# Ten of forty-eight input loads sent as two transfers over uneven parts of the partitions

## The chip, the cores and the metric

The kernel runs on one core of one Trainium2 chip. The metric is the time on the device in microseconds (us), the median over several runs. The core has a matrix engine (PE, with its weight loads, PEld), a vector engine (DVE), a scalar engine (ACT), GpSimd (POOL) and a sequencer, SyncE (SP), that here does nothing but issue transfers. Transfers between the chip's memory and the on-chip memory (128 partitions) are moved by 16 DMA engines.

## What is computed

Two layers in a row: a linear attention with a decaying state (RWKV-6), and a token mixer (HyperMixer) on its output. Batch 4, 8 heads, 768 steps, head size 48; the model width is 8 x 48 = 384.

```
for t in range(S):
    cur = einsum('bhd,bhe->bhde', u[None] * kt, vt)
    y[:, :, t] = einsum('bhd,bhde->bhe', rt, state + cur)
    state = wt[:, :, :, None] * state + einsum('bhd,bhe->bhde', kt, vt)
...
x = y.transpose(0, 2, 1, 3).reshape(B, S, H * D)
W_tok = einsum('bsd,btd->bst', x @ w_q, x @ w_k) / sqrt(d_hyper)
out = maximum(einsum('bst,btd->bsd', W_tok, x), 0.0) @ w_out
```

The four large inputs r, k, v and w (the decay) have the shape (4, 8, 768, 48) in float32, 4.7 MB each; the output is 4.7 MB too.

## The kernel before

The 768 steps of each batch are cut into three units of 256 steps, so there are twelve units, numbered n = 0 to 11; each unit is two chunks of 128. For a unit the kernel needs four inputs: w, k, r and v. Each is loaded by one transfer of 384 KB, so there are 4 x 12 = 48 input loads. A load puts two neighbouring steps on each of the 128 partitions: per partition it moves 8 heads x 2 steps x 48 values, in 8 runs of 384 bytes (two neighbouring steps of a head lie together in memory). The tiles `wg`, `kg`, `rg` and `vg` are rings of four buffers each, so a load may start when the unit four before it has been read from that buffer.

The readers of the loads are: ACT, which takes the logarithm of `wg` (`f_ln`, L378); GpSimd, at times ACT, which casts `kg` and `rg` to 16 bits (`cast16`, L384, recorded under L389); and GpSimd and ACT, which cast `vg` in four quarters into `VB` (`f_V`, L488, recorded under L493). Behind these casts PE transposes k and r, builds the products of each chunk (A), which DVE masks (`AM`, L535), updates the state (`SB`), and forms the unit's output; GpSimd multiplies the values for the present step (`Vd`, L515). After the third unit of a batch the token mixer runs on its rows, and the results are stored.

The order of work is written out by hand: `Plan.add` collects steps, the list `ORDER` says in which order they are issued, and each engine runs its own steps in that order. A step that waits holds all later steps of its engine. All input loads, the weights (`wts`, `wo`) and nearly all stores are issued by SyncE, in the order of `ORDER`. Of the input loads that is: w0 k0 r0 v0 w1 k1 r1 w2 v1 r2 k2 w3, then k4 k3 r3 v2 v3 w4 r4 w5 k5 v4, then, after the weights for q and k, r5 w6 k6 v5 and so on to v11. Each issue on SyncE takes the next of eight semaphores in turn, and waits until the transfer that used this semaphore before it has landed. The small input u is loaded by ACT in two transfers of 4 partitions each (L289).

The load itself is one statement of `load` (L223), called for each unit from the loop at L371. Its argument `e` is the way that the plan hands to a step; for loads it isn't used.

Of the kernel before, what the change touches and what calls it, by code (L numbers as in the profile page):

```python
# [17 lines left out]
def view(t, off, dims, p0=0, pn=128):  # L18

    base = t[ds(p0, pn), ds(off, 1)]  # L20
    return dataclasses.replace(base, ap=[list(base.ap[0])] + [list(d) for d in dims])
# [11 lines left out]
class Plan:  # L33
# [9 lines left out]
    def add(self, key, ways, fn, after=(), buf=None, reads=(), cols=0, mode=0, behind=None,  # L43
            half=-1, more=None):
        s = dict(key=key, ways=ways, way=ways[0], fn=fn, after=list(after), buf=buf,
                 reads=list(reads), cols=cols, mode=mode, behind=behind, half=half,
                 more=more or {}, i=len(self.steps), fills=False, out=False)
        if buf is not None:
            if buf.filler is None:
                buf.filler = s  # L50
                s["fills"] = True
                if buf.tile is None:
                    self.banks.append(buf)
                elif behind is None and buf.before is not None:
                    s["behind"] = buf.before.filler
            elif behind is None:
                s["behind"] = buf.filler
        self.steps.append(s)
        return s
# [77 lines left out]
WARM = 24  # L137
VSW = "PAD"
TURN = (9, 10)


@with_exitstack
def kernel(
# [12 lines left out]
    nc = tc.nc  # L156
    B, H, S, D = r.shape
    C = 128
    U = 2 * C
    NU = S // U  # L160
    NCH = S // C
    NP = H // 2
    D2 = 2 * D
# [56 lines left out]
    km = const([C, 1], F32, "km")  # L220

    def load(b, i, tl, ap, e):
        nc.sync.dma_start(  # L223
            out=view(tl, 0, [[D2, H], [1, D2]]),
            in_=ap[b, :, ds(i * U, U)].rearrange("h (p j) d -> p h (j d)", j=2))

    def pads(e, x):
        y = nc.vector if e == "D" else nc.gpsimd
# [7 lines left out]
    def ring(kind):  # L236
        x = Buf(kind, tiles[kind][used[kind] % RINGS[kind][0]])
        x.before = last.get(kind)
        last[kind] = x
        used[kind] += 1  # L240
        return x
# [7 lines left out]
    def either():  # L249
        return Buf("x")  # L250

    def at(b, dtype=F32):
        x = PS[:, ds(b.bank * 512, 1024 if b.kind == "w" else 512)]
        return x if dtype == F32 else x.bitcast(dtype)

    def copy(e, o, i, by=None):
        if e == "A":
            if by is None:
                nc.scalar.copy(o, i)  # L259
            else:  # L260
                nc.scalar.activation(o, i, ACT.Copy, bias=0.0, scale=by)
        else:
            x = nc.gpsimd if e == "P" else nc.vector
            if by is None:
                x.tensor_copy(o, i)  # L265
            else:
                x.tensor_scalar_mul(o, i, by)
# [56 lines left out]
    def dma(key, fn, after=(), buf=None, reads=()):  # L324
        return add(key, "S", fn, after, buf, reads)
# [35 lines left out]
    def unit(n, batch):  # L361
        b, i = divmod(n, NU)
# [7 lines left out]
        g = {}  # L370
        for name, ap in (("wg", w), ("kg", k), ("rg", r), ("vg", v)):  # L371
            g[name] = ring(name)
            g[name + "L"] = dma((name, n), lambda e, ap=ap, x=g[name].tile: load(b, i, x, ap, e),
                                buf=g[name])

        lw = ring("lw")
# [42 lines left out]
        for cs in fine:  # L419
# [7 lines left out]
            def f_en(e, cs=cs):  # L427
# [3 lines left out]
            x = add(("ep", n, cs[0]), "A", f_ep, [cws, su["kp"]], ep, [cw], cols=w_,  # L431
                    half=-1 if len(cs) > 1 else cs[0])
# [34 lines left out]
        for cs in fine:  # L467
# [7 lines left out]
            def f_KT(e, cs=cs):  # L475
# [3 lines left out]
            x = add(("RT", n, cs[0]), "D", f_RT, [rTs] + [eps[c] for c in cs] + new("ep"), RT, [rt, ep],  # L479
                    cols=512 * len(cs), half=half)  # L480
# [31 lines left out]
        for cs in fine:  # L512
# [5 lines left out]
            x = add(("Vd", n, cs[0]), "PD" if end else "P", f_vd, VBs + [dds], Vd, [VB, dd], cols=len(cs) * DM)  # L518
# [23 lines left out]
        for cs in ([(0,)] if final else fine):  # L542
            def f_kb(e, cs=cs):
                for c in cs:
# [10 lines left out]
            x = add(("kb", n, cs[0]), "eE" if kb.kind == "x" else "E", f_kb,  # L555
                    [KTs[c] for c in cs], kb, [KT], cols=len(cs), mode=dict(e=1, E=0))

            def f_kd(e, cs=cs):
# [3 lines left out]
                else:  # L562
                    x = view(at(kb, BF16), cs[0] * NP * D, [[D, n4], [1024, 2], [1, D]])
                copy(e, view(kd.tile, 64 + cs[0] * 1024, [[256, n4], [128, 2], [1, D]]), x, UNIT)
            x = add(("kd", n, cs[0]), "AD", f_kd, [x] + ([wts["pads"][n]] if n < 2 else []), kd,
                    [kb], cols=DM * len(cs))
# [81 lines left out]
        for p, cs in enumerate(each if end else both):  # L648
# [14 lines left out]
            def f_x(e, c0=c0, nc_=nc_, y=y):  # L663
# [5 lines left out]
                else:  # L669
# [4 lines left out]
                     more=dict(D=([Vds[c] for c in cs], [Vd]), A=([yv], [])))  # L674
            xt, XT = None if n in TURN else either(), ring("XT")

            def f_xt(e, c0=c0, nc_=nc_, xt=xt):
                for dt in range(NK):
                    for k_ in range(nc_):
# [5 lines left out]
                        for hf in range(2):  # L685
                            rows = ds(hf * 64, 64)
                            mm(at(xt, BF16)[:, ds(hf * 1024 + (k_ * NK + dt) * 64, 64)],
                               X.tile[rows, x], ID16[rows, rows], trans=True)
            if n not in TURN:
                xts = add(("xt", n, c0), "eE", f_xt, [xs], xt, [X], cols=nc_, mode=dict(e=1, E=0))  # L690

            def f_XT(e, nc_=nc_, xt=xt, XT=XT):
                if xt.kind == "s":
                    copy(e, XT.tile[:, ds(0, nc_ * DM)], at(xt, BF16)[:, ds(0, nc_ * DM)])
                else:
                    copy(e, view(XT.tile, 0, [[C, NK * nc_], [64, 2], [1, 64]]),
                         view(at(xt, BF16), 0, [[64, NK * nc_], [1024, 2], [1, 64]]))
            if n in TURN:
                XTs = dma(("XT", n, c0), lambda e, XT=XT: nc.sync.dma_start_transpose(
# [24 lines left out]
            if not end:  # L724
                def f_qk(e, f_wk=f_wk, f_wq=f_wq):
# [3 lines left out]
                x = add(("QK", n), "AD", lambda e, qk=qk: copy(  # L729
                    e, QK.tile[:, ds(i * QS, QS)], at(qk)[:, ds(0, QS)]), [qs], QK, [qk], cols=256)  # L730
# [86 lines left out]
    for n in range(N):  # L817
        if n % NU == 0:
            batch = {"k": [], "q": [], "x": []}
        unit(n, batch)  # L820
# [39 lines left out]
```

## Time and profile before

| | |
|---|---|
| median of three runs | 100.72 us (100.42 to 102.55) |
| the profiled execution: time | 99.53 us |
| the profiled execution: span from its first to its last instruction | 97.8 us |
| granted TensorE clock | 1.00 throughout |
| read from memory, written to it | 19.66 MB, 4.72 MB |
| input loads | 48 of 384 KB, issued from 0.8 to 67 us |

The profile's page gives the busy time of each engine with its share of the span, the span in 40 slices of about 2.4 us, the DMA queues (queue 1 has the transfers that SyncE issues, queue 8 fetches instructions), and the chain of work that ended last, followed back from the end. A view by stages gives the same busy times for stretches that one chooses, with the clock, the mean busy share of the 16 DMA engines (above 1 where the packets of one engine overlap) and the GB/s moved. In a timeline a row has the start, the duration, the engine and line, the operation, what it writes and reads, and how often; in brackets stands the idle time ahead of it and what ended it. SPq is SyncE's queue of issues: the duration of an issue holds its wait. The time to landing runs from the start of an issue to the last mark on its semaphore; a landed load leaves one mark for each DMA engine that took part.

### The profile page before, as it was taken

The page shows a single profiled execution, that of the slowest core. Times are in us where ns is not written, and L with a number is a line of the kernel's source. Part 1 is how long each engine was busy: PE and PEld are TensorE (multiplying, and loading weights), DVE is VectorE, ACT ScalarE, POOL GpSimd, SP SyncE. Part 2 cuts the span into 40 slices and gives each one's busy share as a digit, 9 for nine tenths or more (in the row PEclk, how much of TensorE's full clock was granted, in tenths as well). Part 3 has the DMA queues.
Part 4 walks back from the last instruction along what each step waited for, and adds up shares of the span by engine and source line. Part 5 has one row for each costly group of instructions (what it writes and reads, how often), then busy time and mean ns, then how long its engine had stood idle before and what let it go on. Part 6 is the DMA issues. An engine that isn't in the chain of part 4 may idle for free.

```text
span 97.8 us, 4074 instructions
## 1 busy us (share of the span) xinstructions
PE 87.7 (90%) x1710; PEld 67.6 (69%) x1713; DVE 81.7 (83%) x142; ACT 76.0 (78%) x112; POOL 68.1 (70%) x106
## 2 busy tenths in 40 slices
PE   4996888999889899999999999999999999998940
PEld 1354677878677798877788787897787776675410
DVE  5608989999999998999898999899998996384850
ACT  5237988889799799899999999869889856806610
POOL 6659758728799998767999998999968991000000
PEclk9999999999999999999999999999999999999999
DMA  1999999999999999999999999999913695928593
GB/s 29 304 323 325 325 325 299 222 292 315 287 306 247 227 287 215 304 270 245 303 301 308 277 300 294 311 323 248 289 57 132 195 153 150 397 83 322 215 319 112
DMA packets 54914, 25.03 MB, mean 256 GB/s; under 512 B 52592, under 2 KB 53744, under 8 KB 54896
## 3 DMA queue, kind: packets, MB, share of 16 engines
q1 hardware_dynamic: 54736, 24.58, 90.6%
q8 instruction: 13, 0.21, 0.8%
q10 hardware_dynamic: 160, 0.20, 0.6%
q14 instruction: 5, 0.04, 0.1%
HBM read 19.66 MB, written 4.72 MB: 249 GB/s over the span
## 4 chain that ended last, share of the span: by engine, by line
PE 42%; DMA 18%; POOL 18%; DVE 8%; issue 4%; ACT 3%; SPq 3%; POOLq 0%; DVEq 0%; ACTq 0%
PE PS L176 42%; DMA vg<-in_v_dram 12%; POOL VB L493 7%; POOL Vd L515 6%; DMA kg<-in_k_dram 6%; SPq L223 3%; DVE os L265 2%; POOL k L389 2%; POOL KT L476 2%; POOL r L389 2%; DVE RT L471 1%; ACT en L428 1%; DVE AM L535 1%; ACT ep L423 1%; DVE qT L462 1%
## 5 line engine op out<-in xcount | busy, mean ns | idle before, releaser
L535 DVE TENSOR_TENSOR AM<-PS,US 128x1024 bf16<-128x1024 f32 x24 | 28.8, 1218 | 1.0 <-PE PS L176 0.6
L493 POOL CAST VB<-vg 64x384 bf16<-64x384 f32 x42 | 21.1, 503 | 3.2 <-DMA vg<-in_v_dram 0.9
L515 POOL TENSOR_TENSOR Vd<-VB,dd 128x768 bf16<-128x768 bf16 (+1 forms) x14 | 18.0, 1292 | 1.6 <-DVE dd L265 1.1
L428 ACT ACTIVATE en<-PS,km 128x1024 bf16<-128x1024 f32 (+1 forms) x14 | 13.6, 989 | 2.4 <-PE PS L176 2.0
L423 ACT ACTIVATE ep<-PS,kp 128x1024 bf16<-128x1024 f32 (+1 forms) x14 | 13.8, 1003 | 1.4 <-PE PS L176 1.1
L176 PE MATMUL PS<-wo,MX 128*128 128x384 bf16 x72 | 13.5, 326 | 0.5 <-DVE MX L273 0.5
L176 PEld LDWEIGHTS <-KT 48*128 48x128 bf16 (+1 forms) x288 | 10.3, 95 | 3.9 <-issue 1.7
L389 POOL CAST k<-kg 128x768 bf16<-128x768 f32 x11 | 9.0, 824 | 4.5 <-DMA kg<-in_k_dram 4.3
L379 ACT ACTIVATE lw<-wg 128x768 bf16<-128x768 f32 x12 | 10.1, 844 | 2.2 <-DVE kd L230 2.1
L176 PE MATMUL PS<-RT,KT 48*128 48x128 bf16 x192 | 9.2, 217 | 1.2 <-DVE qT L462 0.5
L176 PE MATMUL PS<-CM,lw 64*128 64x128 bf16 (+1 forms) x160 | 9.4, 230 | 0.6 <-DVE ks L265 0.4
L176 PEld LDWEIGHTS <-MX 128*128 128x128 bf16 x72 | 6.2, 97 | 4.9 <-DVE MX L273 1.3
L476 DVE TENSOR_TENSOR KT<-PS,en 128x1024 bf16<-128x1024 bf16 (+1 forms) x10 | 6.3, 631 | 3.7 <-ACT en L428 3.6
L389 POOL CAST r<-rg 128x768 bf16<-128x768 f32 x10 | 8.2, 823 | 1.2 <-DMA rg<-in_r_dram 1.1
L271 ACT ACTIVATE MX<-PS 128x768 bf16<-128x768 f32 (+1 forms) x10 | 7.6, 780 | 1.5 <-PE PS L176 1.4
L471 DVE TENSOR_TENSOR RT<-PS,ep 128x1024 bf16<-128x1024 bf16 (+1 forms) x14 | 8.4, 610 | 0.5 <-PE PS L176 0.3
L462 DVE TENSOR_TENSOR qT<-PS,ks 128x1024 bf16<-128x1024 bf16 x12 | 8.2, 680 | 0.7 <-PE PS L176 0.7
L176 PEld LDWEIGHTS <-lw 64*128 64x128 bf16 (+1 forms) x160 | 6.8, 96 | 2.3 <-issue 0.9
L670 DVE TENSOR_TENSOR X<-PS,Vd 128x768 bf16<-128x768 f32 (+1 forms) x8 | 6.8, 850 | 1.6 <-PE PS L176 1.5
L176 PE MATMUL PS<-ID,r 128*128 128x128 bf16 x96 | 7.4, 220 | 0.8 <-POOL r L389 0.7
L176 PE MATMUL PS<-Z 128*128 128x512 bf16 x16 | 6.5, 523 | 1.2 <-DVE Z L826 1.2
L259 ACT COPY os<-PS 128x768 f32<-128x768 f32 (+1 forms) x9 | 6.2, 694 | 1.8 <-PE PS L176 1.8
(77 smaller groups left out, 189.7 us busy)
## 6 DMA issues: line engine op xcount, KB each, us to landing
wg<-in_w_dram SPq DMA_DIRECT2D x12, 384.0 KB, 5.3
kg<-in_k_dram SPq DMA_DIRECT2D x12, 384.0 KB, 6.0
rg<-in_r_dram SPq DMA_DIRECT2D x12, 384.0 KB, 5.1
vg<-in_v_dram SPq DMA_DIRECT2D x12, 384.0 KB, 5.9
out_dram<-os SPq DMA_DIRECT2D x9, 384.0 KB, 2.6
out_dram<-os SPq DMA_DIRECT2D x5, 192.0 KB, 2.6
wof<-in_moe_w_out_dram SPq DMA_DIRECT2D x1, 576.0 KB, 6.2
out_dram<-os ACTq DMA_DIRECT2D x1, 192.0 KB, 2.3
```

Source lines behind the costliest of these rows:

```text
L176: return nc.tensor.matmul(o, l, rr, start=start, stop=stop, skip_group_check=True, is_transpose=trans)
L271: nc.scalar.activation(o, i, ACT.Relu)
L379: nc.scalar.activation(view(lw.tile, 0, [[64, H], [512, 2], [1, D]]), view(g["wg"].tile, 0, [[D2, H], [D, 2], [1, D]]), ACT.Ln, bias=0.0, ...
L389: op(view(o.tile, 0, [[64, H], [512, 2], [1, D]]), view(g[src].tile, 0, [[D2, H], [D, 2], [1, D]]))
L423: nc.scalar.activation(view(ep.tile, cs[0] * EW + 1, [[2 * EW, NP], [EW, len(cs)], [1, C]]), sums(cs), ACT.Exp, bias=kp, scale=1.0)
L428: nc.scalar.activation(view(en.tile, cs[0] * C, [[U, NP], [C, len(cs)], [1, C]]), sums(cs), ACT.Exp, bias=km, scale=-1.0)
L462: lambda e: nc.vector.tensor_tensor(qT.tile, at(rt, BF16), ks.tile, ALU.mult),
L471: nc.vector.tensor_tensor(slots(RT.tile, cs, C, 0, 64), slots(at(rt, BF16), cs, C, 0, 64), slots(ep.tile, cs, EW, 65, -65), ALU.mult)
L476: on("D" if e == "d" else e).tensor_tensor(plain(KT.tile, cs), plain(at(kt, BF16) if e == "d" else ks.tile, cs), plain(en.tile, cs), ALU.mult)
L493: op(view(VB.tile, c * DM, [[1, DM]], p0=half * 64, pn=64), view(g["vg"].tile, (1 - half) * D, [[D2, H], [1, D]], p0=c * 64, pn=64))
L515: (nc.vector if e == "D" else nc.gpsimd).tensor_tensor(Vd.tile[:, cols], VB.tile[:, cols], view(dd.tile, cs[0] * H, [[1, len(cs) * H], [0, ...
L535: AMs[c] = add(("AM", n, c), "D", lambda e, c=c, A=A: nc.vector.tensor_tensor(view(AM[c].tile, 0, [[C, 8], [1, C]]), view(at(A), 0, [[C, 8 ...
```

## The change

Ten loads, the ones from k of unit 4 to v of unit 4 in the order of issue, are issued as two transfers, over the first and the remaining partitions: 120 and 8, 126 and 2, 117 and 11, 108 and 20, 121 and 7, each pair for two loads. The loop at L371 now hands `load` the letter of the input, by which it looks up the parts; a load that isn't in the table goes as before. Both parts are issued one after the other by SyncE, and a reader of the tile waits for both. Bytes, order, buffers and everything else stay as they are.

```diff
+PARTS = {("k", 4): (120, 8), ("k", 3): (126, 2), ("r", 3): (117, 11), ("v", 2): (108, 20),
+         ("v", 3): (121, 7), ("w", 4): (120, 8), ("r", 4): (126, 2), ("w", 5): (117, 11),
+         ("k", 5): (108, 20), ("v", 4): (121, 7)}
...
     def load(b, i, tl, ap, e):
-        nc.sync.dma_start(
-            out=view(tl, 0, [[D2, H], [1, D2]]),
-            in_=ap[b, :, ds(i * U, U)].rearrange("h (p j) d -> p h (j d)", j=2))
+        p0 = 0
+        for pn in PARTS.get((e, b * NU + i), (C,)):
+            nc.sync.dma_start(
+                out=view(tl, 0, [[D2, H], [1, D2]], p0=p0, pn=pn),
+                in_=ap[b, :, ds(i * U + 2 * p0, 2 * pn)].rearrange("h (p j) d -> p h (j d)", j=2))
+            p0 += pn
...
-            g[name + "L"] = dma((name, n), lambda e, ap=ap, x=g[name].tile: load(b, i, x, ap, e),
+            g[name + "L"] = dma((name, n), lambda e, ap=ap, x=g[name].tile: load(b, i, x, ap, name[0]),
                                 buf=g[name])
```

## The prediction

> **What bounds the kernel now.** I read the page first (busy shares, slices, queues, chain), then the busy times by stage, then SyncE's own issue times, then the chain in order of time with GpSimd's timeline beside it.
>
> ```profile
> PE 87.7 (90%) x1710; PEld 67.6 (69%) x1713; DVE 81.7 (83%) x142; ACT 76.0 (78%) x112; POOL 68.1 (70%) x106
> GB/s 29 304 323 325 325 325 299 222 292 315 287 306 247 227 287 215 304 270 245 303 301 308 277 300 294 311 323 248 289 57 132 195 153 150 397 83 322 215 319 112
> q1 hardware_dynamic: 54736, 24.58, 90.6%
> q8 instruction: 13, 0.21, 0.8%
> PE 42%; DMA 18%; POOL 18%; DVE 8%; issue 4%; ACT 3%; SPq 3%; POOLq 0%; DVEq 0%; ACTq 0%
> ...
> 6.00:14.00 8.00, 6.54 (x98) 4.87 (x98) 5.98 (x11) 6.34 (x11) 5.70 (x12) 1.00 1.17 325
> ...
> 14.00:28.20 14.20, 12.50 (x246) 10.58 (x248) 14.07 (x24) 12.40 (x19) 10.44 (x17) 1.00 1.07 286
> 28.20:46.00 17.80, 17.24 (x399) 14.49 (x398) 17.20 (x29) 16.47 (x24) 15.61 (x20) 1.00 1.01 261
> 46.00:72.00 26.00, 25.31 (x606) 21.33 (x606) 24.66 (x39) 24.26 (x34) 24.74 (x33) 1.00 1.04 284
> 72.00:97.80 25.80, 21.34 (x357) 14.47 (x355) 16.93 (x31) 14.40 (x26) 7.95 (x10) 1.00 0.63 200
> ```
>
> The stage rows give start:end, length, then busy time of PE, PEld, DVE, ACT and POOL, the granted clock, the DMA share and GB/s. Two streams run side by side. The loads move 325 GB/s until 14 us and only 261 to 286 after it. The arithmetic is full behind them: DVE is busy 14.07 of 14.20 us in the stretch in which the ten changed loads are issued, PE 17.24 of 17.80 in the next. So earlier loads have little to give, while later loads can cost.
>
> ```profile
> 0.79 0.46 SPq L223 DMA_DIRECT2D wg<-in_w_dram  x1
> ...
> 12.70 1.15 SPq L223 DMA_DIRECT2D wg<-in_w_dram  x1
> 13.96 2.40 SPq L223 DMA_DIRECT2D kg<-in_k_dram  x1
> 17.62 1.13 SPq L223 DMA_DIRECT2D rg<-in_r_dram  x1
> 22.93 1.60 SPq L223 DMA_DIRECT2D rg<-in_r_dram  x1
> 26.93 1.25 SPq L223 DMA_DIRECT2D vg<-in_v_dram  x1
> 28.23 2.01 SPq L334 DMA_DIRECT2D wqf<-in_moe_w_q_dram  x1
> 33.60 2.43 SPq L223 DMA_DIRECT2D vg<-in_v_dram  x1
> ...
> DMA to landing us min/median/max: 3.4/5.3/6.7
> ```
>
> An issue costs SyncE 0.46 us when nothing is queued and 1.15 us later. 384 KB at 325 GB/s are 1.21 us, just the spacing of the issues (1.15 and a gap of 0.05): SyncE is held back by full DMA queues, not by buffers. Some issues are longer: 2.40, 1.60, 2.01, 2.43. They fall together with instruction fetches, the 13 packets of queue 8, each of which occupies one DMA engine for 0.008 x 16 x 97.8 / 13 = 0.96 us. Read from the packets and the semaphore marks in the trace, which no view prints:
>
> ```
> fetch packets of queue 8 start at 14.73 22.58 28.73 34.32 40.36 45.64 51.58 57.30 62.39 65.85 (and three after the loads)
> w of unit 3, issued at 12.70: fifteen marks from 17.08 to 17.44, the sixteenth at 18.82
> u, two loads of 4 partitions: five marks each, one at once and four later; all other loads leave sixteen
> ```
>
> ```profile
> wg<-in_w_dram SPq DMA_DIRECT2D x1, 384.0 KB, 4.9
> ...
> wg<-in_w_dram SPq DMA_DIRECT2D x1, 384.0 KB, 6.1
> ...
> uR<-in_u_dram ACTq DMA_DIRECT2D x2, 0.8 KB
> ```
>
> The first row is the last wg issue before the first fetch, the second the one at 12.70: 1.2 us later to land, all of it one engine's share. A load counts as landed when its last share has; one engine (E below) carries the fetches and sets the pace. The account closes: 48 x 1.21 us, 2.4 us for the 0.79 MB of weights and ten fetches x 0.96 us make 70.1 us, and the loads run from about 2 to 72 us.
>
> **The change part by part.** (1) Who moves what. One partition of a load on one engine costs 1.21 / 8 = 0.15 us, as a 128-partition load leaves sixteen marks, so 8 partitions an engine. u's 4 partitions left four late marks. I take it that a transfer uses the largest number of engines up to 16 that divides its partitions, counted always from the same end, because both u transfers disturbed the same four engines' rhythm. Then 120, 126, 117, 108 and 121 partitions go on 15, 14, 13, 12 and 11 engines with 8, 9, 9, 9 and 11 each, and the small parts add 1, 1, 1, 2 and 1 on the first 8, 2, 11, 10 and 7. Over the ten loads the first two engines get 104 partitions in place of 80, the next five 102, number 7 (counting from 0) 100, 8 and 9 98, 10 94, 11 to 15 only 70, 52, 34, 16 and 0. So the busiest engine gains 24 x 0.15 = **3.6 us** of work. [...]
>
> (2) What is taken away. If E is one of 11 to 15, its two fetches inside the stretch (14.73 and 22.58) no longer hold the loads: 2 x 0.96 = **-1.9 us**. The stretch ends 3.6 - 1.9 = 1.7 us late. But E is then idle while the others are queued up. The queue's depth: a load lands 4.9 us after its issue and 3.4 at the least, of which 1.21 is its own transfer, so 4.9 - 3.4 + 1.21 = 2.7 us of work wait. That is a lead for E which covers the next two fetches (28.73 and 34.32), another -1.9 us. From about 36 us on the loads are where they were. Its bounds: no lead leaves +1.7 us to the end, a full lead -0.2. E is not among the four engines of u, whose rhythm the 14.73 fetch left alone; that leaves 4 to 15.
>
> (3) What 1.7 us of lateness cost. The tightest consumer is GpSimd:
>
> ```profile
> 21.74 1.59 POOL L389 CAST k<-kg 128x768 bf16<-128x768 f32 x2 [1.77 <-DMA kg<-in_k_dram]
> 24.80 3.29 POOL L493 CAST VB<-vg 64x384 bf16<-64x384 f32 x6 [0.70 <-DMA vg<-in_v_dram]
> 28.17 2.91 POOL L515 TENSOR_TENSOR Vd<-VB,dd 128x768 bf16<-128x768 bf16 x2
> 33.11 1.06 POOL L493 CAST VB<-vg 64x384 bf16<-64x384 f32 x2
> ...
> 38.53 0.82 POOL L389 CAST k<-kg 128x768 bf16<-128x768 f32 x1 [0.31 <-DMA kg<-in_k_dram]
> 42.62 0.82 POOL L389 CAST r<-rg 128x768 bf16<-128x768 f32 x1 [0.67 <-DMA rg<-in_r_dram]
> ...
> vg<-in_v_dram SPq DMA_DIRECT2D x1, 384.0 KB, 5.9
> ```
>
> v of unit 4, issued at 26.93, lands at 32.8 and is cast at 33.11: 0.3 us of slack, so GpSimd starts it 1.4 us late, with k's and r's casts and Vd queued behind it, and PE and DVE behind those. GpSimd waited 0.31 and 0.67 us for loads at 38.53 and 42.62; these waits shrink by its own lateness once the loads are back on time, 1.0 us. What stays is 1.4 - 1.0 = +0.4 us. Ahead of that the first loads of the stretch come earlier (the 1.77 us wait for k shortens), but DVE, full there, doesn't use it: 0.
>
> (4) Small things. Ten more issues cost SyncE at least 0.46 us each, 4.6 us in 14 us, hidden by its being held back 1.15 us a load anyway; were the queues empty, they would cost that much. A second part is a second semaphore to wait for:
>
> ```profile
> L223 SPq EVENT_SEMAPHORE  x26: 17/17/28, 13.9 to 66.9; - x26
> ```
>
> 17 ns each; ten, some twice in front of casts, are 0.2 us at most on any engine, and I count +0.2. The eight semaphores in turn now cover four split loads rather than eight: an issue waits for the landing of the fourth load before it. Four loads take at least 4.8 us and land after 4.9 to 6, so this binds barely, if at all: 0, at worst 1 us (6.0 - 4.8).
>
> Sum: +0.4 + 0.2 = +0.6 us on the profiled execution's 99.53, which is 100.1. The median of the runs, 100.72, stands 1.2 above that execution, so **101.3 us**.
>
> [...]
>
> **The rivals.** *B, E is one of engines 4 to 10.* Then the fetches stay and E itself gets 14 to 22 partitions more, 2.1 to 3.3 us, with no lead to win it back; nothing later repays it, as E paces the loads to 72 us. Less 0.3 of slack, plus 0.2: about +2.9, **103.6 us**. For it: seven of the twelve places left. Against it: five of twelve would be relieved.
> [...]
>
> *C, faster.* Relief ends the load waits themselves:
>
> ```profile
> 18.80 5.88 DMA vg<-in_v_dram
> ...
> 32.66 5.82 DMA kg<-in_k_dram
> ...
> 38.52 6.05 DMA vg<-in_v_dram
> ```
>
> These three pieces of the chain exceed an undisturbed 4.9 us by 0.98, 0.92 and 1.15, together 3.0. If E stays ahead so long and the idle engines make no new laggard, up to 3.0 us go: **98.3** with 2.4 of them. It decides once E's lead lasts past 38 us and the first engines' 3.6 us fit into their idle time (they run at 286 of 325 GB/s, 12% of 14.2 = 1.7 us). Against it: 1.7 is less than 3.6, and DVE has 0.13 us to spare.
>
> *D, the parts don't divide as I think.* If a part of odd size ran on one engine, 121 partitions would take 18 us, and the kernel would lose over 50 us. If the rows went evenly over all sixteen, nothing would move: 100.9.
>
> **How the numbers follow.** A (E relieved, small loss) 0.47: five of twelve is 0.42, raised a little as a guess, since a queue that serves no loads is likelier put at an end of the row than in its middle. B 0.36, C 0.12, D 0.05. A's own range is 100.2 (loss 0, a little gained early) to 102.6 (no lead, semaphores binding). Two per cent is about what a measurement of this kernel can tell from no change: below 98.7 or above 102.7. Faster: 0.07 of C. Slower: 0.29 of B, 0.03 of A, 0.03 of D, 0.35. Same: 0.58. The range leaves out half of C, the top of B and the bad half of D: 99.2 to 104.2.
>
> **What would show it.** In the changed profile: for (1), the issue rows of the ten loads spaced about 1.6 us a load and GB/s near 11/16 to 15/16 of before in 16 to 30 us; for (2), k of units 4 and 3 landing about a microsecond earlier, v of unit 4 one to two later than 32.8, and no long issue at 28 and 33 us; for (3), GpSimd's wait at 21.7 shorter and one of about 1.4 us at the VB cast near 33; for B, the last load landing near 75 us in place of 72. The prediction is wrong if E lies in the overloaded part, if the engines' shares aren't what I worked out, or if PE and DVE turn out to have slack that takes the whole lateness.

## The result, and the profile after

The changed kernel is slower: 106.93 us in the median of four runs (106.06 to 109.09), against 100.57 us for the kernel before beside it. The ratio is 1.057, with a 95% interval of 1.049 to 1.065. Forecast were 101.3 us, in a range of 99.2 to 104.2. Ratios here and below leave out runs in which the chip was in a slower state, while the medians are over all runs.

The page of the changed kernel: span, busy times, GB/s in 40 slices (of 2.7 us here), queues, shares of the chain.

```profile
span 107.4 us, 4097 instructions
...
PE 95.1 (89%) x1713; PEld 72.0 (67%) x1713; DVE 83.1 (77%) x142; ACT 76.4 (71%) x112; POOL 68.1 (63%) x106
...
GB/s 35 317 325 324 274 244 186 197 201 217 190 204 251 264 232 292 272 305 301 299 298 236 309 251 301 316 299 251 207 0 153 140 232 74 322 124 288 151 303 140
...
q1 hardware_dynamic: 54776, 24.58, 82.2%
q8 instruction: 13, 0.21, 0.7%
...
PE 49%; SPq 22%; DMA 12%; DVE 7%; POOL 3%; issue 3%; ACT 1%; POOLq 0%; DVEq 0%
```

From the seventh slice to the twelfth (16 to 32 us) the rate is 186 to 217 GB/s; before it was 222 to 315 in this time. The chain now starts with SyncE's issues, which had 3% of it and have 22%. The bytes are the same, 24.58 MB.

The view of DMA issues of the same kernel (tile, queue, how often, size) says which loads these are:

```profile
vg<-in_v_dram SPq DMA_DIRECT2D x9, 384.0 KB
...
wg<-in_w_dram SPq DMA_DIRECT2D x2, 363.0 KB
kg<-in_k_dram SPq DMA_DIRECT2D x2, 363.0 KB
rg<-in_r_dram SPq DMA_DIRECT2D x2, 363.0 KB
vg<-in_v_dram SPq DMA_DIRECT2D x2, 363.0 KB
...
vg<-in_v_dram SPq DMA_DIRECT2D x1, 324.0 KB
...
vg<-in_v_dram SPq DMA_DIRECT2D x1, 60.0 KB
...
vg<-in_v_dram SPq DMA_DIRECT2D x2, 21.0 KB
```

At 3 KB a partition, 363 KB are 121 partitions, 324 are 108, 60 are 20 and 21 are 7. There is no row of 360 KB (120 partitions), 378 (126) or 351 (117), and every input is cut alike: one load as 108 and 20, two as 121 and 7. So not ten loads are cut as the table says, but twelve: all four inputs of unit 2 as 108 and 20, of units 3 and 4 as 121 and 7. The reason stands in the diff's last line. The function handed to the plan binds `ap` and `x` when it is made (`ap=ap`), but not `name`; it looks `name` up when the plan is carried out. By then the loop over the inputs has ended, `name` is "vg" for every load, and each load asks the table for ("v", n). The table has this for units 2, 3 and 4; its seven entries for w, k and r are never read. The section on the change above describes the table, and is wrong about what is issued.

The profiled execution above ran with a granted TensorE clock of 0.83 in the mean, so its times by stage are not comparable with those of before. A second profile of the same kernel (e6_after_again below, span 105.3 us) has the full clock but for 6.8 us (hence 0.95 and 0.85 in the first two rows below), and is read from here on. Its stages, in the columns used before:

```profile
14.00:28.20 14.20, 9.75 (x176) 8.28 (x178) 10.57 (x18) 9.62 (x12) 6.81 (x9) 0.95 0.81 198
28.20:46.00 17.80, 15.37 (x316) 12.64 (x314) 14.30 (x22) 12.68 (x19) 13.93 (x18) 0.85 0.96 237
46.00:72.00 26.00, 25.43 (x623) 21.29 (x619) 24.61 (x41) 24.05 (x36) 23.38 (x32) 1.00 1.06 285
72.00:97.80 25.80, 25.28 (x484) 19.06 (x482) 20.78 (x35) 19.59 (x31) 15.06 (x20) 1.00 0.74 212
```

The loss arises between 14 and 46 us. DVE, which was busy 14.07 of 14.20 us in the first stretch, is busy 10.57; the loads move 198 GB/s in place of 286, and the mean busy share of the DMA engines falls too, from 1.07 to 0.81, so they are idle more. From 46 to 72 us everything is as full as before, so nothing is won back, and 4 us of PE's work are pushed past 72 us (25.28 busy there, 21.34 before). SyncE's issues of this kernel:

```profile
15.97 1.99 SPq L228 DMA_DIRECT2D wg<-in_w_dram  x2
18.07 3.89 SPq L228 DMA_DIRECT2D kg<-in_k_dram  x4
22.01 2.06 SPq L228 DMA_DIRECT2D rg<-in_r_dram  x2
24.12 4.16 SPq L228 DMA_DIRECT2D vg<-in_v_dram  x4
...
34.19 3.31 SPq L228 DMA_DIRECT2D vg<-in_v_dram  x2
...
74.09 1.42 SPq L228 DMA_DIRECT2D vg<-in_v_dram  x1
```

A cut load takes SyncE about 2.0 us (x4 are two loads in 3.89 or 4.16) in place of about 1.2. v of unit 4 is issued at 34.19 in place of 26.93, the last input load at 74.09. That row of the kernel before is

```profile
66.99 1.09 SPq L223 DMA_DIRECT2D vg<-in_v_dram  x1
```

so the last load is 7.1 us late, and the span 105.3 - 97.8 = 7.5 us longer. (On the chip of the second profile the kernel before issued this load at 68.75 us in e5_before_again, which makes it 5.3 us late.) GpSimd's timeline and the chain of the changed kernel's second profile show who waits:

```profile
25.40 1.59 POOL L395 CAST k<-kg 128x768 bf16<-128x768 f32 x2 [4.12 <-DMA kg<-in_k_dram]
28.49 0.83 POOL L395 CAST r<-rg 128x768 bf16<-128x768 f32 x1 [1.49 <-DMA rg<-in_r_dram]
...
40.84 1.06 POOL L499 CAST VB<-vg 64x384 bf16<-64x384 f32 x2 [0.47 <-PE PS L179]
```

```profile
29.00 1.39 SPq L228
30.49 5.80 DMA rg<-in_r_dram
36.32 0.84 ACT r L395
...
42.85 11.78 PE PS L179 x257
```

The wait for k ahead of 25.40 is 4.12 us where it was 1.77, and the cast of v of unit 4 starts at 40.84 in place of 33.11. The chain goes through issues of SyncE to 29.00 + 1.39 = 30.39, a load of r and its cast, and then mostly through PE, with one more load of r at 56.02. The loads set the pace until 36 us, and the full engines carry the lateness to the end.

### The profile page after: what moved, and what is told of

Its sections match the earlier page's. It is cut to its first block, busy times and chain, and to the rows that moved or that the text cites. A ratio compares the mean times of both kernels' runs of the same rounds, so it can differ in the third digit from the quotient of the medians.

```text
span 107.4 us, 4097 instructions
## 1 busy us (share of the span) xinstructions
PE 95.1 (89%) x1713; PEld 72.0 (67%) x1713; DVE 83.1 (77%) x142; ACT 76.4 (71%) x112; POOL 68.1 (63%) x106
## 3 DMA queue, kind: packets, MB, share of 16 engines
q1 hardware_dynamic: 54776, 24.58, 82.2%
## 4 chain that ended last, share of the span: by engine, by line
PE 49%; SPq 22%; DMA 12%; DVE 7%; POOL 3%; issue 3%; ACT 1%; POOLq 0%; DVEq 0%
PE PS L179 49%; SPq L228 22%; DMA vg<-in_v_dram 12%; POOL VB L499 2%; DVE AM L541 2%; DVE os L271 2%; DVE MX L279 1%; POOL k L395 1%; ACT kd L267 1%; DVE RT L477 1%; DVE qT L468 1%; DVE KT L482 1%; ACT os L265 0%; DVE SB L608 0%; DVE dd L271 0%
## 5 line engine op out<-in xcount | busy, mean ns | idle before, releaser
L179 PE MATMUL PS<-wo,MX 128*128 128x384 bf16 x72 | 15.0, 355 | 0.3 <-DVE MX L279 0.3
L179 PEld LDWEIGHTS <-KT 48*128 48x128 bf16 (+1 forms) x288 | 11.6, 101 | 2.7 <-issue 1.6
L179 PE MATMUL PS<-CM,lw 64*128 64x128 bf16 (+1 forms) x160 | 10.1, 243 | 0.8 <-ACT lw L385 0.5
L179 PE MATMUL PS<-ID,r 128*128 128x128 bf16 x96 | 8.2, 235 | 2.6 <-POOL r L395 2.6
L179 PE MATMUL PS<-ID,k 128*128 128x128 bf16 x96 | 8.2, 235 | 2.4 <-POOL k L395 2.4
L179 PE MATMUL PS<-RT,KT 48*128 48x128 bf16 x192 | 10.0, 232 | 0.1
L179 PE MATMUL PS<-Z 128*128 128x512 bf16 x19 | 7.8, 501 | 1.2 <-DVE Z L832 1.2
L179 PEld LDWEIGHTS <-k 128*128 128x128 bf16 x96 | 6.4, 104 | 3.5 <-POOL k L395 2.9
```

The costliest lines, as they stand in the source:

```text
L179: return nc.tensor.matmul(o, l, rr, start=start, stop=stop, skip_group_check=True, is_transpose=trans)
```

## The experiments

Two causes were weighed. *Shares*: a load of 128 partitions leaves sixteen marks on its semaphore, of which the last is its landing; the parts of 121 and 7 partitions leave eleven and seven (their times stand in the next section). If each of these marks is the share of one engine, an engine can have 11 partitions of the one part and 1 of the other, 12 in place of 8, and the busiest engine has more to move. *Cutting*: two transfers, over few partitions, cost something of their own, whatever the shares. The experiments ran in three groups, each beside the kernel before on one chip. The kernel before itself took 103.15 us (median) in the first, 100.84 in the second and 101.81 in the third, so only ratios are compared. The intervals are 0.01 to 0.02 to each side; the kernel before, entered as an experiment (e5_before_again), came out at 0.988 (0.980 to 0.996) of itself, so a difference of 1% is not read.

**What the late binding does.** First the loads that the table names, with the letter bound:

```diff
-lambda e, ap=ap, x=g[name].tile: load(b, i, x, ap, name[0]),
+lambda e, ap=ap, x=g[name].tile, name=name: load(b, i, x, ap, name[0]),
```

> Each load looks up its own letter, so the ten loads of the table are split and no others. Theory (shares of the engines): the busiest engines get 24 partitions more (3.6 us at 0.15 us each), engine 7, if it is the one that fetches, 20 more (3.0 us); the load stream ends 3.0 to 3.6 us late and the kernel takes about 3.3 us more than before, ratio 1.03 (1.02 to 1.04). If the fetches are on one of engines 11 to 15 instead: 1.00 to 1.015. Rival (each further transfer costs by itself, through its issue and its semaphore): ten of twelve further transfers as in the changed kernel, so 1.05. The 8-partition part should have one share later than the others if engine 7 fetches, and none if 8 or 9 does.

Ratio 1.013 (1.003 to 1.023), 104.52 us. The same kernel once more in the third group:

> The ten loads of the table alone, each looking up its own letter, again, where the kernel before runs steadily. By the shares: 24 partitions more on the busiest engines, 3.6 us, ratio 1.03 to 1.04; part of that could be won back from the engine that fetches (1.00 to 1.015). Changed packets (120 and 8 gave 217 GB/s with the engines full) would add up to 1 us: at most 1.05.

Ratio 1.023 (1.012 to 1.034), 104.12 us. So the change as its table describes it is probably slower too, by 1 to 2%, which is little more than the 1% that is not read. Both ratios lie below the 1.03 that the shares alone were expected to give. Then the letter bound and the table written out for the loads that the changed kernel issues (the binding as in e1_bound here and in all that follow, but for e5 and e6):

```diff
+PARTS = {(x, n): (108, 20) if n == 2 else (121, 7) for x in "wkrv" for n in (2, 3, 4)}
```

> The table written out for what the changed kernel is thought to issue: all four loads of unit 2 as 108 and 20, of units 3 and 4 as 121 and 7, each load looking up its own letter. If that reading is complete, this is the changed kernel again: ratio 1.049 to 1.065, the busiest engines 44 partitions late (6.6 us), engine 7 by 36 (5.4 us), the last load issued about 6 us later than before. If something else in the change costs time, it is faster than that.

Ratio 1.029 (1.019 to 1.039), 106.23 us, span 104.7. The ratio is below the 1.049 to 1.065 expected: the time is the changed kernel's, 106.9, but the kernel before was 2.6 us slower in this group, and why is open. The load stream is the changed kernel's too. Its last load, at 74.09 there, is issued here at 74.45:

```profile
74.45 1.10 SPq L226 DMA_DIRECT2D vg<-in_v_dram  x1
```

e4 took 1.7 us more than e1_bound on the same chip, but the two intervals overlap. The changed kernel itself, with no edit, and the kernel before, in the second group:

> The changed kernel, unchanged, beside the kernel before on one chip, with a profile. If the loss is the lateness of the load stream (last load issued about 6 us later), the ratio is 1.04 to 1.065 on any chip; if a granted clock below 1 made much of it, it falls to 1.03 or less where both have the same clock.

> The kernel before, unchanged, to have its profile on the chip on which the next three run: ratio 1.00 (0.99 to 1.01), packets of the loads about as in the profile of before (107% DMA share at 288 GB/s between 18 and 28 us).

The changed kernel: ratio 1.068 (1.058 to 1.077), 108.33 us; the kernel before: 100.70 us. So the loss was 5.7% in the first measurement and is 6.8% in this one. The clock is not tested by this: it was 0.965 to 0.968 in the changed kernel's runs and 0.990 to 1.000 in those of the kernel before (the last section returns to it).

**Which of the two causes.** The same twelve loads, cut between heads, so that both transfers go over all 128 partitions: as many issues and semaphores, equal shares by that count, all partitions.

```diff
-        p0 = 0
-        for pn in PARTS.get((e, b * NU + i), (C,)):
+        h0 = 0
+        for hn in PARTS.get((e, b * NU + i), (H,)):
             nc.sync.dma_start(
-                out=view(tl, 0, [[D2, H], [1, D2]], p0=p0, pn=pn),
-                in_=ap[b, :, ds(i * U + 2 * p0, 2 * pn)].rearrange("h (p j) d -> p h (j d)", j=2))
-            p0 += pn
+                out=view(tl, h0 * D2, [[D2, hn], [1, D2]]),
+                in_=ap[b, ds(h0, hn), ds(i * U, U)].rearrange("h (p j) d -> p h (j d)", j=2))
+            h0 += hn
+PARTS = {(x, n): (4, 4) for x in "wkrv" for n in (2, 3, 4)}
```

> The same twelve loads as two transfers each, but cut by heads, four and four, over all 128 partitions: as many transfers, issues and semaphores as in the changed kernel, with every engine's rows as before. Number of transfers: 1.02 or more (112 and 16 gave 1.022). Shares and placement of the rows on the engines: 0.99 to 1.01, with the packets' DMA share and GB/s as before.

Ratio 0.993 (0.986 to 1.000), 100.59 us. Twelve more transfers cost nothing here. Next the halves of the partitions, with equal shares, by the author's count four partitions an engine:

```diff
+PARTS = {(x, n): (64, 64) for x in "wkrv" for n in (2, 3, 4)}
```

> The same twelve loads as 64 and 64 partitions, four rows an engine in each half: shares even, as with 112 and 16. If a transfer that doesn't give each engine its usual eight rows makes the packets longer (as the DMA share of 1.16 at 263 GB/s with 112 and 16 suggests), the ratio is 1.02 to 1.05 and 325 GB/s are not reached with the engines full. If only the shares and the number count, it is the same as the cut by heads.

Ratio 1.031 (1.022 to 1.039), 104.40 us. So cutting by partitions does cost something with equal shares, about 3%. The changed kernel, with unequal shares, lost 3.7 points more on the same chip (1.068 against 1.031, the intervals apart). The view of DMA queues from 14 to 24 us shows that these are two different things, which need not add up. Its first row has the packets, MB and rate; its second the packets, MB and time of queue 1 as a share of 16 engines. The kernel before, the changed kernel (e6), e7_heads and e8_64_64:

```profile
DMA packets 7429, 2.84 MB, mean 284 GB/s; under 512 B 7427, under 2 KB 7427, under 8 KB 7427
...
q1 hardware_dynamic: 7427, 2.81, 105.2%
```

```profile
DMA packets 5356, 2.05 MB, mean 205 GB/s; under 512 B 5354, under 2 KB 5354, under 8 KB 5354
...
q1 hardware_dynamic: 5354, 2.02, 78.8%
```

```profile
DMA packets 7307, 2.75 MB, mean 275 GB/s; under 512 B 7305, under 2 KB 7305, under 8 KB 7305
...
q1 hardware_dynamic: 7305, 2.72, 103.7%
```

```profile
DMA packets 6139, 2.30 MB, mean 230 GB/s; under 512 B 6138, under 2 KB 6138, under 8 KB 6138
...
q1 hardware_dynamic: 6138, 2.29, 122.2%
```

The share times 16 engines times 10 us over the packets is the time of one packet: 1.052 x 160 us / 7427 = 22.7 ns before, 23.5 in the changed kernel, 22.7 in e7, 31.9 in e8. In e8 the share is 122.2%, and each packet takes 40% longer. In the changed kernel the packets are nearly as short as before, and the engines are idle more: 78.8% in place of 105.2%. That fits unequal shares. (From 22 to 26 us its packets, read one by one, take 26.8 ns, so some of the other cost is there as well.)

Two transfers over disjoint halves of the partitions are not merely useless in e8, they cost 3%. And what costs here is which rows a transfer covers, since as many transfers of the same size, 192 KB, cost nothing in e7.

Two more splits of the twelve loads, 112 and 16 (equal shares again) and 120 and 8 (nine partitions on eight engines, eight on seven, none on the last), both by the author's count:

```diff
+PARTS = {(x, n): (112, 16) for x in "wkrv" for n in (2, 3, 4)}
```

> The twelve loads that the changed kernel split, each as 112 and 16 partitions: two uneven transfers, but both divide by 16, so every engine keeps its 8 partitions. Theory (shares): within 1% of before (0.99 to 1.01). Rival (number of transfers, issues and semaphores): as slow as the changed kernel, 1.05 to 1.065.

```diff
+PARTS = {(x, n): (120, 8) for x in "wkrv" for n in (2, 3, 4)}
```

> The same twelve loads as 120 and 8: engines 0 to 7 get 9 partitions, 8 to 14 keep 8, engine 15 gets none. Theory with the fetches on engine 7: 12 partitions more, 1.8 us, ratio 1.01 to 1.025, and the 8-partition part has one late share. If engine 15 fetched, the ratio would be 0.97 to 1.005 and no share of it late. Rival (number of transfers): 1.05 to 1.065.

They ran in the first group: ratios 1.022 (1.015 to 1.029) and 1.027 (1.019 to 1.035). Shares that are equal by this count do not save the split, and a difference from e4_explicit (1.029) in the same group isn't shown, as the intervals overlap. The packets from 14 to 24 us, e2's rows and then e3's:

```profile
DMA packets 6588, 2.49 MB, mean 249 GB/s; under 512 B 6586, under 2 KB 6586, under 8 KB 6586
...
q1 hardware_dynamic: 6586, 2.46, 105.2%
```

```profile
DMA packets 5876, 2.22 MB, mean 222 GB/s; under 512 B 5875, under 2 KB 5875, under 8 KB 5875
...
q1 hardware_dynamic: 5875, 2.21, 117.3%
```

That is 25.6 ns a packet in e2 and 31.9 in e3: engines busy at 105.2% and 117.3%, and longer packets, as in e8. With shares that are equal by that count the loads end late as well. The last load of e8 and of e2:

```profile
72.97 0.60 SPq L226 DMA_DIRECT2D vg<-in_v_dram  x1
```

```profile
73.24 1.10 SPq L226 DMA_DIRECT2D vg<-in_v_dram  x1
```

That is 6.0 and 6.2 us after the 66.99 of before, nearly the 7.1 of the changed kernel, while e7 has 68.19. So the lateness alone doesn't tell the two causes apart; the busy share of the engines and the length of the packets do. How the changed kernel's loss divides between them is not shown.

**Which loads, and where.** Unit 2's four loads alone, units 3's and 4's eight alone, and the twelve splits moved to the last three units:

```diff
+PARTS = {(x, 2): (108, 20) for x in "wkrv"}
```

> Only the four loads of unit 2 split, 108 and 20: 12 partitions more on the busiest engines, 1.8 us; ratio 1.01 to 1.025. If the loss came from the eight splits of 121 and 7 alone: 1.00.

```diff
+PARTS = {(x, n): (121, 7) for x in "wkrv" for n in (3, 4)}
```

> Only the eight loads of units 3 and 4 split, 121 and 7: 32 partitions more, 4.8 us; ratio 1.035 to 1.05. With the run above it adds up to the changed kernel (about 1.06 to 1.07) if the shares add.

```diff
+PARTS = {(x, n): (108, 20) if n == 9 else (121, 7) for x in "wkrv" for n in (9, 10, 11)}
```

> The twelve splits of the changed kernel moved to units 9, 10 and 11, the last twelve input loads: the load stream ends as late as in the changed kernel (about 6 us) but only its last part is late. If late loads cost through the casts behind them, v of unit 11 with 5 us to spare and r and w with 1.3 us soften it: 1.02 to 1.05. If the loads' end had slack, 1.01 or less; if each split costs the same wherever it stands, 1.06 to 1.07.

e11_units34: ratio 1.032 (1.013 to 1.050), 106.25 us, at the lower edge of what was expected. The eight loads cut as 121 and 7 alone cost as much, within the intervals, as all twelve did in the first group (1.029). e10_unit2 (102.44 us, 99.85 to 103.08) and e12_late (108.87 us, 104.89 to 109.44) are too widely spread for a ratio. e10 is inconclusive. e12 is slower, since its lowest time, 104.89, is above the highest of the kernel before, 103.64, so the end of the loads hasn't the slack that would hide it; by how much is not shown. In e12's profiled execution the last load is issued at 78.50 us and the span is 106.7, which speaks against a softer loss at the end, but doesn't settle it.

## Why the prediction was wrong, step by step

**The step that failed is "(1) Who moves what".** It took the parts of each load from the table, "over the ten loads". What it took for the number of engines agrees with the number of marks. Read from the semaphore marks in the traces, for w of unit 3 in the two profiles of the changed kernel:

```
first profile    121 partitions: eleven marks, 19.80 to 20.27, the last at 21.14   7 partitions: seven marks, 20.06 to 20.39
second profile   121 partitions: eleven marks, 19.41 to 20.15, the last at 20.77   7 partitions: six marks, 19.61 to 20.27, the seventh at 21.02
```

108 partitions left twelve, 20 ten, and in the bound kernels 120, 126 and 117 left 15, 14 and 13: in each of these parts the largest divisor of its partitions up to 16. In the first profile each part left one more mark soon after its issue, as u's loads did (at 16.74 and 17.34 for the two parts above), so one mark for each engine that took part, as the section on the profile before has it, holds at most for the others. That those are one engine's share each fits the engines' busy share of 78.8% in place of 105.2%, but no view names the engine of a mark, and that the engines are counted from the same end each time is not shown. By that reading the input was wrong. As issued, unit 2's loads give each of the first ten engines 9 + 2 = 11 partitions, and those of units 3 and 4 give the first seven 11 + 1 = 12, where they had 8. That is 4 x 3 + 8 x 4 = 44 partitions more, not 24, and 44 x 0.15 = 6.6 us in place of 3.6. The last load came 7.1 us late in the second profile (6.05 in the first), which fits the price of a partition but doesn't confirm it, as e8 and e2 are 6.0 and 6.2 us late with shares that are equal by the author's count. For the loads that were meant, one sign of this step did come true: in e9 the loads move 236 GB/s between 14 and 28.2 us, 0.83 of the 286 of before, within the 11/16 to 15/16 that was forecast.

The diff's last line shows the late binding, and the prediction had it in view. No rival doubted that the change does what it says: D asks only how a part divides over the engines, not which loads look up a part. A rival that asked what the table returns when the load runs would have caught it.

**"(2) What is taken away" was wrong too, and this was the choice between A and B.** The changed kernel can't test it, since its loads differ; e1 and e9 have the loads that the prediction meant. By A their loads are back on time after 36 us. In e9 the last one is issued late all the same:

```profile
71.57 1.10 SPq L228 DMA_DIRECT2D vg<-in_v_dram  x1
```

That is 4.6 us after the 66.99 of the first profile of before, and 2.8 us after the 68.75 of e5's; in e1 it is 73.60. Nor do the first loads of the stretch come earlier, as A had it; GpSimd's wait for k is longer, not shorter:

```profile
22.43 1.60 POOL L395 CAST k<-kg 128x768 bf16<-128x768 f32 x2 [2.50 <-DMA kg<-in_k_dram]
```

It was 1.77 us. So no relief of 1.9 us and no lead shows.

The choice itself was badly put. If a part counts its engines from the same end each time, a late last mark in a part of k engines puts the laggard among the first k. After the second fetch of the stretch (after the first in the last row) the marks read:

```
e9, fetch at 22.96             11 partitions of r of unit 3: ten marks, 22.97 to 23.65, the last at 25.32   20 of v of unit 2: ten marks, 24.69 to 25.40
e1, fetch at 22.38             20 of v of unit 2: nine marks, 24.29 to 25.34, the last at 26.30
first profile, fetch at 25.49  121 of r of unit 3: ten marks, 24.95 to 26.23, the last at 28.09   20 of v of unit 2: ten marks, 27.34 to 28.20
first profile, fetch at 15.12  20 of k of unit 2: nine marks, 17.45 to 18.06, the last at 19.40
```

By that reading the laggard in e9 is the eleventh engine, number 10; in e1 it is among the first ten. In the first profile of the changed kernel it is among the first ten after one fetch and number 10 after the next, though in the marks further up it isn't among the first seven; in the second profile it is. So the delay doesn't stay with one engine E, as the prediction had it, and in these cases it lay in the loaded part, not in 11 to 15, where A needed it. (For the first fetch of e9 and e1 the marks don't tell.) Nor is it always engine 7, on which e3's and e4's expectations count, as number 10 is another. The exclusion of u's four engines is not shown, since the marks name no engine.

**"(3) What 1.7 us of lateness cost"** failed with it. It let the lateness shrink in the waits for later loads, which needs these loads on time. They were as late as the others. The first part of the step held: in e9 v of unit 4 lands 4.7 us late (at 37.57 in place of 32.84), and GpSimd casts it 4.67 us after the 33.11 of before:

```profile
37.78 1.06 POOL L499 CAST VB<-vg 64x384 bf16<-64x384 f32 x2 [1.57 <-PE PS L179]
```

**"(4) Small things"** held: e7 has twelve more issues, semaphores and waits, and a ratio of 0.993.

**What was missing** is the price of rows that don't cover all partitions, about 3% in e8 and 2% in e2, where the shares are equal by the author's count. No step had it.

**The rivals.** B came nearest in its working, since it lets nothing be won back. With 44 in place of its 14 to 22 partitions it gives 100.72 + 6.6 - 0.3 + 0.2 = 107.2 us, where 106.93 was measured. That is partly luck, as B has no price for the cut itself, and that its engine E was the reason is not shown. For the ten loads that were meant, the measured 1.013 and 1.023 would be 102.1 to 103.0 us on the 100.72 of before, between A and B. That lies in the forecast range, but with the relief of (2) missing and the price of the cut left out, so a hit would have been luck too. C needed earlier loads, and there were none. Both halves of D are out by the marks: 121 partitions left eleven, neither one nor sixteen.

## What to carry to other kernels

Before costing a table of cases, find out which entry each call looks up when it runs: a function made in a loop sees the loop's last value of a name that isn't bound to it. Count the marks that a transfer leaves: where its parts left twelve or fewer in place of sixteen, the DMA engines were busy at 78.8% in place of 105.2%, and the lateness of the loads stayed to the end. If a load must be cut, try a cut in which each piece covers all partitions: it had a ratio of 0.993 here, and the cut into halves of the partitions 1.031.

## What the runs showed of the hardware that was not expected

**Packets took longer in splits whose transfers cover a part of the partitions**, although they have the same 384 bytes: 31.9 ns for 64 and 64 and for 120 and 8, and 25.6 for 112 and 16, against 22.7. For the changed kernel's 108 and 20 and 121 and 7 they took 23.5, with the engines busy at 78.8%. e8 moved 230 GB/s against 284 before; e7, which covers all partitions with each transfer, has packets of 22.7 ns, 275 GB/s and no loss. What makes the packets longer is not shown.

**The granted TensorE clock was 0.50 for 3.4 or 6.8 us in the changed kernel and in some of the experiments.** In the changed kernel's second profile, a stretch cut out of the stages:

```profile
28.00:31.40 3.40, 2.53 (x36) 2.20 (x35) 1.91 (x4) 1.56 (x4) 1.84 (x3) 0.50 0.79 188
```

It follows a stretch (24 to 28 us) in which PE is busy for only 2.35 of 4.00 us:

```profile
24.00:28.00 4.00, 2.35 (x41) 2.11 (x38) 1.98 (x3) 2.29 (x3) 1.59 (x2) 0.85 0.82 180
```

The clock column (the third from the end) reads 0.50 in the first of these rows, and 1.00 in the kernel before throughout. The traces' record of the clock, which no view prints, has it at half from 26.77 to 33.60 us here, and for 3.41 us in e2, e4, e8 and e9. Whether PE's idleness is the reason is not shown, nor what sets these lengths. In the second profile the chain runs through SyncE's issues and a load of r until 36.3 us, past the end of the half clock, so little of that loss is the clock's. The changed kernel took 106.18 and 106.06 us in two runs at a mean granted clock of 0.963 and 0.984, and e2_112_16 took 105.23, 105.33, 104.81 and 105.40 us at 0.982, 1.000, 0.999 and 1.000. But e11_units34 took 104.10 us in a run at 1.000 and 105.63 in one at 0.978, so that the clock costs nothing in any of these kernels is not shown.
